# Recurrent attention beside a windowed attention layer: layer B's V, scores and PV in 32-wide TensorE tiles, layer A in tiles of 64 tokens

## The chip, the cores and the metric

One core of a Trainium2 chip runs the whole program. The metric is the device time of one execution in microseconds (us). A profile of one execution gives every instruction's start and end on TensorE (PE, its weight loads PEld), VectorE (DVE), ScalarE (ACT), GpSimd (POOL) and the queues, and the clock that was granted to TensorE.

## The reference

```python
x = A_x                                    # 1 x 2048 x 576, bfloat16
x = x + A(layernorm(x))                    # layers 1 and 3: 32 heads of 18, each token sees
x = x + B(layernorm(x))                    #   itself and 7 earlier tokens, 2 apart
x = x + A(layernorm(x))
x = x + B(layernorm(x))                    # layers 2 and 4: 32 heads of 128
# B, for each of 64 segments of 32 tokens:
h = concat([mem, xs])                      # 8 memory rows + 32 rows of x
q, k, v = h @ Wq, h @ Wk, h @ Wv
p = softmax(mask(q @ k.T * scale)); o = (p @ v) @ Wo
mem = o[:, :8]; outs.append(o[:, 8:])      # the next segment needs mem
```

Layer B is a recurrence: 64 segments, one after the other. Both B layers run together as two "lanes" of one step, the second a few segments behind the first, with 80 columns (2 x 40) on TensorE.

## The kernel before

Some words first. SBUF and PSUM are the memories in which the program keeps its tiles; all its matmuls write to tiles in PSUM. HBM holds its inputs, its results and A's weights. The columns of a matmul are those of the operand that it streams (80 for most of B's). "Scores" are Q x K^T, "PV" is the product of the softmax P with V, which gives O.

The weights of B stay in SBUF. A step of B is a fixed list of blocks; TensorE's order is laid down when the program is built. Between B's blocks a budget lets blocks of layer A in ("generators" that yield a block of matmuls or a gap of time). A's weights aren't kept beside B's: each block of 160 KB is loaded from HBM into a ring of six buffers when it is needed.

```python
def stage_c(g):                    # 4 heads: V transposed back to rows, scores, softmax
    psV = ...                      # matmul(psV[:, hh, :], lhsT=v^T, rhs=ident)
    for hh in range(4):
        nc.tensor.matmul(psS[:, hh, :], lhsT=q, rhs=k, start=True, stop=False)
        nc.tensor.matmul(psS[:, hh, :], lhsT=self.ident[0:NC2, 0:NC2], rhs=self.m80b[:, :], ...)  # mask
    ...                            # max (VectorE), exp (ScalarE, one per head), sum, P = e / sum (GpSimd)
def stage_e(g): ...                # P transposed by TensorE, copied by ScalarE
def stage_g(g): ...                # O = V x P^T
def oproj(g): ...                  # 6 x 80 columns for each head
# --- cut: A's budget
self.a_budget = min(self.a_budget + dt * cfg["a_share"], cfg["a_burst"])   # 0.25, 1.5
while self.agens and self.a_budget > 0:
    ...
    self.a_budget -= cfg["a_blk"]                                          # 0.3 a block
# --- cut: layer A, tiles of TT = 128 tokens
nc.vector.tensor_copy(out=kT[:, :, 0:HALO], in_=hk[:, 0])   # 14 columns of the tile before
nc.vector.tensor_copy(out=vT[:, :, 0:HALO], in_=hk[:, 1])
```

## Time and profile before

| before | |
|---|---|
| median of 3 | 3384.12 us (3382.23 to 3387.86) |
| busy, of the span of 3384.5 us | PE 84%, PEld 78%, DVE 56%, ACT 44%, POOL 44% |
| mean granted clock | 0.971 |
| loads of A's weight blocks | 640 of 160 KB |

Busy shares say which engine leads; the list of waits says for what it stands still. From that list for TensorE (engine, line waited at, engine and line waited for: us in all, times, longest us):

```profile
PE b_psO L624 <- ACT b_PT L616: 70.6, 119, 2.7
PE b_psO L624 <- DVE b_OT L630: 47.3, 81, 0.6
```

```profile
DVE a_kT L298 <- POOL a_prod L335: 66.9, 30, 6.3
```

Inside the steps TensorE's largest waits are for B's own P and O copies; its one long wait for A's weights, 90.0 us, lies before the first step. The line of VectorE's list looks harmless: VectorE, copying the 14 halo columns of K, waits for GpSimd.

### The profile page before, as it was taken

What the parts mean: (1) busy time and instruction counts of PE and PEld (TensorE: products, weight loads), DVE (VectorE), ACT (ScalarE), POOL (GpSimd) and SP (SyncE); (2) the same over time, 40 slices, a digit from 0 to 9 for tenths busy, and PEclk for the clock granted to TensorE, in tenths of its full rate; (3) what the DMA queues carried; (4) which work ended last, traced back from release to release, by engine and by line L of the source; (5) the groups of instructions that cost most, each with busy time, mean ns of one, the idle gap of its engine ahead of it and who ended that gap; (6) DMA issues with size and microseconds to landing.
All of it is one profiled execution on the core that took longest, in us unless ns stands there. A gap on an engine that the chain in (4) does not pass through costs nothing. (4 is left out here: it accounts for less than half of the span.)

```text
span 3384.5 us, 146469 instructions
## 1 busy us (share of the span) xinstructions
PE 2854.0 (84%) x64880; PEld 2627.9 (78%) x64880; DVE 1894.2 (56%) x4387; ACT 1498.5 (44%) x4729; POOL 1474.9 (44%) x2546
## 2 busy tenths in 40 slices
PE   0488888888888988888888888898888898989887
PEld 0388778887888878888878778887888888878887
DVE  2255655655665555555555556565555565656554
ACT  0244444444444444444444444444444444444443
POOL 3455545454554544354545455454535351515111
PEclk9799999999999999999999999999999999999999
DMA  8222112121222222222212122212222120201000
GB/s 290 68 60 73 53 50 63 37 78 47 65 56 65 57 56 57 66 59 62 65 46 70 44 63 56 65 56 56 57 64 59 31 68 13 67 12 50 14 16 10
DMA packets 246960, 198.35 MB, mean 59 GB/s; under 512 B 120884, under 2 KB 230516, under 8 KB 244788
## 3 DMA queue, kind: packets, MB, share of 16 engines
q1 hardware_dynamic: 142724, 163.81, 16.3%
q10 hardware_dynamic: 100352, 6.30, 1.9%
q0 software_dynamic: 3248, 18.88, 1.5%
q8 instruction: 507, 8.31, 1.0%
q14 instruction: 129, 1.06, 0.1%
HBM read 156.02 MB, written 32.90 MB: 56 GB/s over the span
## 5 line engine op out<-in xcount | busy, mean ns | idle before, releaser
L538 PE MATMUL b_psr<-hT,wq 128*128 128x80 bf16 x9216 | 790.3, 201 | 61.4 <-DVE hT L688 17.3
L538 PE MATMUL b_psr<-hT,wv 128*128 128x80 bf16 x9216 | 765.3, 202 | 0.0
L538 PE MATMUL b_psr<-hT,wk 128*128 128x80 bf16 x9216 | 761.7, 202 | 0.0
L603 POOL TENSOR_TENSOR b_P<-b_sm,b_ssum 80x320 bf16<-80x320 bf16 x504 | 361.1, 718 | 915.6 <-DVE b_ssum L601 490.3
L597 ACT ACTIVATE b_sm<-b_psS,b_nmx 80x80 bf16<-80x80 f32 x2304 | 579.0, 323 | 222.2 <-DVE b_nmx L582 152.1
L538 PEld LDWEIGHTS <-wq 128*128 128x128 bf16 x9216 | 555.5, 100 | 102.4 <-issue 93.6
L644 PE MATMUL b_psY<-b_OT,wo 128*128 128x80 bf16 x13824 | 613.6, 208 | 0.0
L644 PEld LDWEIGHTS <-wo 128*128 128x128 bf16 x13824 | 577.7, 104 | 8.0 <-issue 3.0
L545 ACT CAST b_qkv<-b_psr 128x480 bf16<-128x480 f32 x576 | 321.8, 559 | 542.3 <-PE b_psr L541 541.0
L547 DVE CAST b_qkv<-b_psr 128x480 bf16<-128x480 f32 x576 | 374.2, 650 | 275.9 <-PE b_psr L541 270.4
L538 PEld LDWEIGHTS <-wk 128*128 128x128 bf16 x9216 | 513.1, 100 | 0.5 <-issue 0.2
L538 PEld LDWEIGHTS <-wv 128*128 128x128 bf16 x9216 | 509.8, 100 | 1.7 <-issue 1.6
L616 ACT CAST b_PT<-b_psT 80x320 bf16<-80x320 f32 x576 | 243.8, 423 | 523.5 <-PE b_psT L612 504.5
L600 DVE TENSOR_REDUCE b_ssum<-b_sm 80x4 f32<-80x320 bf16 x576 | 275.9, 479 | 354.7 <-ACT b_sm L597 324.5
L541 PE MATMUL b_psr<-hT,wk_r 128*128 128x80 bf16 x2304 | 464.7, 202 | 0.0
L541 PE MATMUL b_psr<-hT,wv_r 128*128 128x80 bf16 x2304 | 464.1, 201 | 0.0
L541 PE MATMUL b_psr<-hT,wq_r 128*128 128x80 bf16 x2304 | 463.6, 201 | 0.0
L569 PE MATMUL b_psS<-b_qkv 128*80 128x80 bf16 x2304 | 364.9, 206 | 98.1 <-ACT b_sm L597 36.2
L335 POOL TENSOR_TENSOR a_prod<-a_t,a_kT 128x1024 bf16<-128x1024 bf16 x160 | 317.2, 1996 | 134.8 <-ACT a_t L312 86.4
L572 PE MATMUL b_psS<-m80b,ident 80*80 80x80 bf16 x2304 | 358.6, 204 | 0.0
L587 DVE CAST b_V<-b_psV 80x512 bf16<-80x512 f32 x504 | 341.7, 678 | 22.9 <-PE b_psV L559 22.7
L569 PEld LDWEIGHTS <-b_qkv 128*80 128x80 bf16 x2304 | 253.5, 118 | 106.4 <-DVE b_qkv L547 69.6
(140 smaller groups left out, 5208.3 us busy)
## 6 DMA issues: line engine op xcount, KB each, us to landing
a_w<-wA_blk SPq DMA_DIRECT2D x640, 160.0 KB, 2.7
x1T<-xres SPq DMA_DIRECT2D x16, 320.0 KB, 3.0
d2T<-b_stg SPq DMA_DIRECT2D x64, 80.0 KB, 1.6
xres<-x1T SPq DMA_DIRECT2D x16, 320.0 KB, 3.3
xres<-d2T SPq DMA_DIRECT2D x16, 320.0 KB, 2.9
x3T<-xres SPq DMA_DIRECT2D x16, 320.0 KB, 3.5
d4T<-b_stg SPq DMA_DIRECT2D x64, 80.0 KB, 1.6
xres<-x3T SPq DMA_DIRECT2D x16, 320.0 KB, 3.3
```

Source lines behind the costliest of these rows:

```text
L335: e_prod.tensor_tensor(out=prod[:], in0=qT[:, c, :].unsqueeze(1).to_broadcast([P, AW, T]), in1=win(kT, c), op=ALU.mult)
L538: last = nc.tensor.matmul(ps[:, hh, wi, :], lhsT=wt[:, kc, h * P:(h + 1) * P], rhs=hT[:, kc, :], start=(kc == 0), stop=False)
L541: last = nc.tensor.matmul(ps[:, hh, wi, :], lhsT=wr[:, hr * P:(hr + 1) * P], rhs=hT[:, 4 + h // (HB // 2), :], start=False, stop=True)
L545: nc.scalar.copy(out=sb[:], in_=ps[:])
L547: nc.vector.tensor_copy(out=sb[:], in_=ps[:])
L569: mm = nc.tensor.matmul(psS[:, hh, :], lhsT=t_[:, hh % 2, 0, :], rhs=t_[:, hh % 2, 1, :], start=True, stop=False)
L572: last = nc.tensor.matmul(psS[:, hh, :], lhsT=self.ident[0:NC2, 0:NC2], rhs=self.m80b[:, :], start=False, stop=True)
L587: nc.vector.tensor_copy(out=V[:], in_=psV[:])
L597: nc.scalar.activation(out=sm[:, hh, :], in_=psS[:, hh, :], func=ACT.Exp, bias=nmx[:, hh:hh + 1], scale=1.0)
L600: nc.vector.tensor_reduce(out=ssum[:], in_=sm[:], axis=AX.X, op=ALU.add)
L603: (nc.vector if crit else nc.gpsimd).tensor_tensor(out=Pm[:], in0=sm[:], in1=ssum[:].unsqueeze(2).to_broadcast([NC2, 4, NC2]), op=ALU.mult)
L644: last = nc.tensor.matmul(psY[:, mb, :], lhsT=self.wo[:, c0:c0 + P], rhs=OTs[g][:, hh, :], start=(ocount[0] == 1), stop=(ocount[0] == 6 * HB))
```

## The change

The intent is less work on TensorE and fewer dependent copies: four 32-wide tiles work at once in V, scores and PV; V comes straight from x as rows (no transposes); P is transposed on VectorE; the x columns go through PV in this step and through the output projection in the next one, so that only the 16 memory columns are urgent. For this the softmax takes all 128 partitions. Layer A's tiles shrink from 128 to 64 tokens, the lanes' delay from 8 to 6 segments (70 steps, not 72).

```diff
-TT = 128
+T = 64
+NS = T // SEG
--- cut
-                psV = self.ps_r.tile([NC2, 4, P], F32, name="b_psV", tag="r")
-            psT = self.ps_a.tile([P, 4, NC2], F32, name="b_psT", tag="TO")
--- cut
+    def vpass(self, t, b, engines):
+            for kc in range(5):
+                for c in range(4):
+                    mm.append(nc.tensor.matmul(ps[c * 32:(c + 1) * 32, :], lhsT=l, rhs=w, start=(kc == 0), stop=(kc == 4)))
--- cut: score_m, score_x, pv_m, pv_x in groups of four tiles
+        nc.vector.transpose(out=pt[:].rearrange("p i b q -> p (i b q)"), in_=e[:].rearrange("p i k -> p (i k)"))
--- cut: the order of a step
+        for g in range(11):
+            seq.append((self.qk, t, g))
+            if g == 6:
+                seq += [(self.vpass, t, 1, ("act", "dve")), (self.score_m, 0), (self.score_x, 0)]
+        seq += [(self.vpass, t, 0, ("act", "act")), (self.score_m, 1), (self.score_x, 1), (self.pv_m, 0),
+                (self.oproj, 0, 12), (self.pv_m, 1), (self.oproj, 12, 16), (self.oproj, 16, 24), (self.oproj, 24, 32),
+                (self.mem_out, t), (self.x_out, t - 1), (self.pv_x,)]
--- cut: A's budget, a block of weights costs 0.15
-        self.a_budget = min(self.a_budget + dt * (cfg["a_share"] if share is None else share), cfg["a_burst"])
+        self.owed = min(self.owed + us, 2.0)
+SHARE = 0.18
```

## The prediction

> **What bounds the kernel now.** I read the page first (busy shares, slices, chain), then the stretches of two steps without and three with layer-A work, then the groups of instructions by shape, the list of waits, and the timeline of single steps.
>
> The page:
>
> ```profile
> PE 2854.0 (84%) x64880; PEld 2627.9 (78%) x64880; DVE 1894.2 (56%) x4387; ACT 1498.5 (44%) x4729; POOL 1474.9 (44%) x2546
> ...
> PE b_psY L644 5%; PE b_psr L538 4%; ACT b_sm L597 3%; DVE b_qkv L547 2%; PE b_psS L569 1%; ACT b_qkv L545 1%; PE b_psr L541 1%; DVE b_V L587 1%; PE b_psO L624 1%; PE b_psT L612 1%; ACT b_PT L616 1%; DVE b_ssum L600 1%; DVE b_nmx L582 1%; PE a_psqkv L308 1%; DVE b_OT L630 1%
> ```
>
> TensorE leads with 84%, and the chain that ended last runs from engine to engine. The program is a recurrence: 72 steps of layer B (64 segments and a delay of 8), each needing the memory columns that the last one put out. Stretches of the timeline, all engines (start and end, length, busy time and count of each engine, clock, DMA):
>
> ```profile
> 0.00:149.20 149.20, 20.74 (x156) 12.16 (x157) 32.80 (x76) 9.35 (x19) 67.18 (x153) 0.87 0.61 201
> 149.20:3375.00 3225.80, 2832.59 (x64719) 2615.28 (x64718) 1859.76 (x4308) 1489.15 (x4710) 1407.69 (x2393) 0.98 0.19 52
> ...
> 3257.80:3296.50 38.70, 34.54 (x833) 32.18 (x833) 20.44 (x47) 16.94 (x56) 5.02 (x7) 1.00 0.02 5
> ...
> 1616.00:1662.40 46.40, 40.04 (x883) 36.35 (x883) 29.22 (x68) 21.47 (x66) 25.29 (x54) 0.96 0.22 58
> ```
>
> About 149 us of loading and the first A tile, 3226 us of steps (44.8 each), 10 us of tail. A step with no A work takes 38.7 us, one with it 44 to 46. A step has 832 matmuls of layer B: 480 projections, 192 output projections, and 160 for V transposes, scores, masks, P transposes and PV. From start to start they are about 36 ns apart (56 for the 32 of N=128), so B's TensorE work is 800 x 36 + 32 x 56 = 30.6 us; A adds on average 3.7 us (counts by start gaps). The remaining 8 us without A and 10 to 11 with it are waits. Where they lie, from the timeline of the step without A:
>
> ```profile
> 3288.80 1.89 PE L644 MATMUL b_psY<-b_OT,wo 128*128 128x80 bf16 x48
> ...
> 3292.40 0.32 PE L612 MATMUL b_psT<-ident,b_P 80*80 80x80 bf16 x4
> 3292.81 0.42 ACT L616 CAST b_PT<-b_psT 80x320 bf16<-80x320 f32 x1 [1.45 <-PE b_psT L612]
> 3293.28 0.30 PE L624 MATMUL b_psO<-b_PT,b_V 80*128 80x80 bf16 x4 [0.56 <-ACT b_PT L616]
> 3293.62 0.49 DVE L630 CAST b_OT<-b_psO 128x320 bf16<-128x320 f32 x1 [3.01 <-PE b_psO L624]
> 3294.17 0.30 PE L624 MATMUL b_psO<-b_PT,b_V 80*128 80x80 bf16 x4 [0.58 <-DVE b_OT L630]
> ```
>
> 48 matmuls less the 0.2 us of one's length give 36 ns each; then TensorE waits 0.56 us for each copy of P or O: the softmax chain of the last head groups has too little work laid over it.
>
> [...] A's logits already use four 32-column tiles:
>
> ```profile
> 1691.11 0.29 PE L340 MATMUL a_psL<-a_prod,epad 128*32 128x256 bf16 x4
> 1714.19 0.39 PE L373 MATMUL a_psB<-a_e,epadT 32*128 32x256 bf16 x4
> ```
>
> Four matmuls of N=256 are done in 0.29 us, where one takes 0.285: they start 3 ns apart. In single records about 130 ns pass into and 210 ns out of such a group, of which 107 is streaming: some 100 ns per change of mode. The second line has two row tiles twice: the second pair starts 120 ns after the first, so a group costs its streaming time plus 13 ns. [...] (min/median/max in ns):
>
> ```profile
> L603 DVE TENSOR_TENSOR b_P<-b_sm,b_ssum x72: 424/489/1458, 187.7 to 3367.6; 80x320 bf16<-80x320 bf16 x72
> ```
>
> [...]
>
> **The change, TensorE work of a B step.** Q and K: 320 x 36 ns = 11.5 us. V: 6 half passes of 5 groups of four N=512 tiles, (512/2.4 + 13) ns a group, 6 x 1.13 = 6.8 (before 160 x 36 ns plus 32 transposes of 56 = 7.5). Scores with masks: groups of four at 36 + 13 = 50 ns; mask groups 146 and 173 ns; 2 x (0.35 + 0.57) = 1.8 (before 64 x 36 = 2.3). P transposes: gone (1.15). PV: 12 + 12 + 24 groups of 50 ns = 2.4, more than the 1.15 before. Output: 160 x 36 = 5.8 (192 before: 6.9). Nine changes of mode: 0.9. Sum 29.2 us, against 30.6. So the tiles themselves save only 1.4 us a step. A tiles of 64 tokens: per tile 100 matmuls of N=64 (29 ns, 2.9 us), 10 of N=128 for the norms (0.6), logits 0.6, spread 0.5, transposes 0.2: 4.8 us x 64 / 70 steps = 4.4 us (before 3.7). Together 33.6 us a step, before 34.3.
>
> **What is worth more: waits.** The softmax takes all 128 partitions, with 16 heads an instruction: exp 576 x 4 pieces of 0.32 us become 280 of about 0.45; the copy of P^T on ScalarE goes; V is copied from two passes that don't need memory. The x columns' PV and the V pass of the next step's second lane stand between the last output matmul and the next Q/K: 1.2 + 2.3 us over the 0.6 us in which memory returns. That wait (0.5 us) is gone. VectorE gets more: per step 5 QK copies 3.3, one V copy 0.7, max/add/sum/reciprocal/multiply/transpose 2 x 2.6 + 2 x 2.5, O copies 2.2, memory 0.6, together 17 us, plus A 7.7: 25 of some 39 us. No engine but TensorE is at its limit.
>
> I followed two steps by hand through the built order, with these durations. Four waits came out. (a) The first PV's copy of O stands on VectorE behind max, add, sum and reciprocal of the second score half, ready 3.4 us after those scores; TensorE is there after 1.6: 1.8 us before the output matmuls. (b) PSUM: Q/K, V, scores and A's products now share three buffers; behind the first score half a Q/K group waits for an exp or for a copy that VectorE does after the softmax: 2 to 3 us. (c) A's spread and PV share one buffer of four banks: 1.6 us where they meet. (d) Less than 0.5 elsewhere. The two walks ended at 40.6 and 41.2 us; both were dense in A work, and without A I get 34. I take 33.6 + 5.2 = 38.8.
>
> **Forced tiles.** In the built order of TensorE, from step 17 on every sixth step, eight times, logits, spread, output and norm of one A tile stand back to back: the next segment needs it. The chain: softmax 2.0, spread and its copies 2.8, V multiplies 1.6, GpSimd adds 4.5 (slope of the before kernel's adds), residual and norm 1.5: some 11 us of waiting each.
>
> **Sum.** Start 140 (A tile smaller, weights the same), 62 steps x 38.8 = 2406, 8 x 50 = 400, tail 15 (one more output projection, then the last tile): 2961, so 2960 us, 12.5% less. Of the gain of 424, two steps fewer give 90, the rest is waits.
>
> **Rivals.** R1, waits fully hidden: 33.6 us a step, 70 x 33.6 + 155 = 2507, or 2600 with forced tiles. For it: the work is there to fill with. Against: TensorE runs in one fixed order, and the before kernel with the same freedom keeps 10 us. R2, VectorE becomes the bound in the score stretches, as its two-input multiplies are shut out by GpSimd (1400 instead of 489 ns in 16 of 72 cases) and every copy queues behind them: 3 us more a step, 3170. Against: only 3 to 5 of its instructions a step have two SBUF inputs. R3, tile groups of small N don't keep 50 ns[...]. The trace shows groups of four only singly, so it can't be ruled out. R4, weight traffic doubles (1280 blocks of 160 KB instead of 640, some 205 MB): the mean DMA share is 19%, so 40% at most; hidden.
>
> **Range and chances.** A walk of dependent waits may miss by 2.5 us a step: 2760 to 3160. Slower than before would need 46 us a step, R2 and R3 together and more: faster 0.94, same 0.04, slower 0.02.
>
> **What would show it.** Steps of about 39 us and eight of about 50; V groups 226 ns apart; TensorE's wait for the first O copy near 1.8 us; waits of Q/K matmuls on VectorE copies; no wait at the step's border. Wrong if small groups are slower than 50 ns, if the transposes take over 1 us, or if the waits at shared PSUM are under 3 us or over 8.

## More of the kernel before

The page's row of the clock (tenths, 40 slices) is full:

```profile
PEclk9799999999999999999999999999999999999999
```

## The result, and the profile after

| | before | after |
|---|---|---|
| median | 3383.18 us (3381.19 to 3387.86) | 3582.65 us (3575.53 to 3590.58) |
| granted clock | 0.971 | 0.880 |
| steps | 72 | 70 |

The kernel became slower: ratio 1.0588 (95% interval 1.0563 to 1.0613). Ratios here are the mean time of one kernel's fast runs over that of the other's of the same rounds, so not quite the ratio of the medians. The result lies 623 us above the prediction. The page after:

```profile
PE 2646.4 (74%) x73360; PEld 2213.0 (62%) x73360; DVE 1583.8 (44%) x3949; ACT 1051.7 (29%) x2317; POOL 1007.2 (28%) x1007
...
PEclk9998889898979879897897988989899799978899
```

No engine is busier than before: the time went into waiting, and the clock has holes. TensorE's and VectorE's largest waits inside the steps now:

```profile
PE b_psY L601 <- DVE OT L560: 181.2, 93, 4.3
PE a_psqkv L290 <- DMA a_w<-wA_blk: 111.5, 119, 3.7
...
PE b_psqk L452 <- DVE b_qk L461: 69.0, 40, 6.7
PE a_psY L373 <- POOL a_o L367: 57.3, 9, 6.4
```

```profile
DVE a_k L284 <- POOL a_big L310: 221.3, 55, 9.3
```

Three of the five are layer A's. The tiles themselves do what they should; from the timeline of one step (start us, us, engine, line, operation, count):

```profile
1595.76 1.05 PE L484 MATMUL b_psv<-wv,hT 128*32 128x512 bf16 x16
1596.63 0.39 PE L484 MATMUL b_psv<-wv_r,hT 128*32 128x512 bf16 x4
...
1598.07 0.32 PE L516 MATMUL b_psm<-b_qk 128*32 128x80 bf16 x16
1598.21 0.34 PE L530 MATMUL b_psx<-mask_x,ident 128*32 128x384 bf16 x4
```

From start to start, 16 V matmuls take 0.87 us, 217 ns for a group of four; 16 score matmuls take 0.14 us, 35 ns a group.

**A ledger of TensorE's time.** I split the time from start to start of its matmuls, from the first step (149.2 us before, 132 us after) to the last matmul, into: columns at full clock (columns / 2.4 ns, a group of four tiles counted once; at full clock matmuls of 80, 128 and 256 columns start 36, 56 and 109 ns apart in the trace before, 2.4 columns a ns between them, and at half clock those of 80 and 128 start 67 and 107 ns apart in the trace after, 1.2 a ns; the clock records of both have only the levels 1.0 and 0.5); what half clock adds; gaps of over 150 ns beyond that, by the matmul that ends them; and the rest. (The parts exceed the time, by up to 2.2% in the tables of this document, where neighbouring matmuls overlap; trust the rest least.)

| us | length | columns | half clock | gaps ahead of A | gaps ahead of B | rest |
|---|---|---|---|---|---|---|
| before | 3231 | 2294 | 61 | 91 | 510 | 276 |
| after | 3443 | 1941 | 278 | 411 | 538 | 320 |

The work fell by 353 us. Gaps ahead of A's blocks took 320 of it back, the clock 217. By steps: those with A work take 46.9 us in the mean, except the eight in which a whole A tile was forced through in front of the step (75.9 us); predicted were 38.8 and 50.

### The profile page after: what moved, and what is told of

Same layout as the page of the kernel before. It is cut to its first block, busy times and chain, and to the rows that moved or that the text cites.

```text
span 3579.8 us, 159066 instructions
## 1 busy us (share of the span) xinstructions
PE 2646.4 (74%) x73360; PEld 2213.0 (62%) x73360; DVE 1583.8 (44%) x3949; ACT 1051.7 (29%) x2317; POOL 1007.2 (28%) x1007
## 5 line engine op out<-in xcount | busy, mean ns | idle before, releaser
L452 PE MATMUL b_psqk<-hT,wq 128*128 128x80 bf16 x8960 | 729.9, 209 | 171.6 <-DVE b_qk L461 69.0
L452 PE MATMUL b_psqk<-hT,wk 128*128 128x80 bf16 x8960 | 729.0, 209 | 0.0
L601 PE MATMUL b_psY<-OT,wo 128*128 128x80 bf16 (+1 forms) x11360 | 551.8, 222 | 182.0 <-DVE OT L560 181.2
L484 PE MATMUL b_psv<-wv,hT 128*32 128x512 bf16 x6720 | 476.1, 405 | 43.7 <-DVE b_qk L461 31.3
L454 PE MATMUL b_psqk<-hT,wq_r 128*128 128x80 bf16 x2240 | 467.5, 209 | 0.1
L454 PE MATMUL b_psqk<-hT,wk_r 128*128 128x80 bf16 x2240 | 467.0, 208 | 0.0
L310 POOL TENSOR_TENSOR a_big<-a_q,a_k 128x1024 bf16<-128x1024 bf16 (+1 forms) x192 | 320.1, 1692 | 134.6 <-ACT a_k L296 132.8
L290 PE MATMUL a_psqkv<-a_xn,a_w 128*128 128x64 bf16 x4800 | 260.9, 202 | 130.4 <-DMA a_w<-wA_blk 111.5
L454 PEld LDWEIGHTS <-wq_r 128*128 128x128 bf16 x2240 | 234.4, 105 | 0.0
L454 PEld LDWEIGHTS <-wk_r 128*128 128x128 bf16 x2240 | 234.0, 104 | 0.0
```

What stands on the lines that cost most here:

```text
L290: mm = [nc.tensor.matmul(ps[:, c, :], lhsT=w[:, kc, :], rhs=xn[:, kc, :], start=(kc == 0), stop=(kc == 4)) for kc in range(5)]
L310: nc.gpsimd.tensor_tensor(out=big[:, c0:c0 + nb], in0=qT[:, c0:c0 + nb].unsqueeze(2).to_broadcast([P, nb, AW, T]), in1=win(kT, c0, nb), op ...
L452: mm.append(nc.tensor.matmul(ps[:, hh, wi, :], lhsT=wt[:, kc, h * P:(h + 1) * P], rhs=hT[:, kc, 0:W80], start=(kc == 0), stop=False))
L454: mm.append(nc.tensor.matmul(ps[:, hh, wi, :], lhsT=wr[:, (h % 16) * P:(h % 16 + 1) * P], rhs=hT[:, 4 + h // 16, 0:W80], start=False, stop ...
L484: mm.append(nc.tensor.matmul(ps[c * 32:(c + 1) * 32, :], lhsT=l, rhs=w, start=(kc == 0), stop=(kc == 4)))
L601: mm.append(nc.tensor.matmul(self.psY[:, mb, c0:], lhsT=self.wo[:, w0:w0 + P], rhs=self.OT[:, h, c0:], start=(h == 0 and mb == 0), stop=(h ...
```

## The experiments

Every edit is on the changed kernel unless another is named.

**1. The queue of the weight loads.** B's loads and stores stand on the same queue as A's weight loads; they go to ScalarE's.

```diff
-            self.nc.sync.dma_start(out=hT[:, :, XC[lane]:XC[lane] + SEG], in_=self.xnT[lane][:, s])
+            self.nc.scalar.dma_start(out=hT[:, :, XC[lane]:XC[lane] + SEG], in_=self.xnT[lane][:, s])
```
(and the two stores alike)

> Only edit: the x loads, the stores of the layer-B output and the final stores are issued from ScalarE's queue, so that A's weight loads stand behind fewer waits in the SyncE queue. Weight theory (286 us more than streaming time in A's projections, because their blocks stand in one queue behind stores that wait for the step's end): the wait of A's projections falls from 286 us above streaming to under 150, half-clock share from 0.25 to 0.18-0.21, time 3350 to 3480. Rival (the pace of issue and a ring of six buffers sets the wait, not the queue's order): within 1% of 3583.

Measured: 3623.37 us, ratio 1.0703 (1.0687 to 1.0719), slower than the change itself. TensorE's wait for weights at A's projections stayed at 111.5 us in all, so waits at the head of that queue are not what holds the weights up. What became longer are the waits of Q/K matmuls for ScalarE, from 91 to 142 us; the likely reason, not tested, is that ScalarE's own instructions now stood behind those transfers' waits.

**2. PV earlier.** PV of the first half goes ahead of the second half's scores, so that its O copy isn't behind their softmax on VectorE.

```diff
-(self.score_m, 1), (self.score_x, 1), (self.pv_m, 0),
+(self.pv_m, 0), (self.score_m, 1), (self.score_x, 1),
```

> Only edit: the first PV half is put before the second score half, so that its copy stands ahead of that softmax on VectorE. Stall theory: the wait of the output projection for the copy of O (128 us above streaming) nearly goes, and the clock drops that it sets off (33 of 136) too: time 3583 minus 125 minus about 60, 3370 to 3440, half-clock share about 0.20. Rival (TensorE then only waits at the second PV instead, as the softmax of the second score half has less over it): wait moves, time over 3520.

Measured: 3549.37 us, ratio 1.0482 (1.0441 to 1.0523): 33 us. Most of the wait moved: ahead of the output projection it fell from 181 to 77 us for VectorE's copies, and 90 us of such waits appeared ahead of PV. It is a small term.

**3. Does the clock count?** 28 idle multiplications fill the wait for the first O copy, once with 112 columns each, once (control) with 4.

```diff
-                (self.oproj, 0, 12),
+                (self.warm, 28, 112), (self.oproj, 0, 12),
```

> Only edit: 28 idle matmuls of 112 columns (1.4 us at full clock) into spare columns of the output bank, in the wait between the first PV and the output projection; nothing else moves. Clock theory[...]: drops set off at that place (33 of 136) mostly go, half-clock share 0.25 to about 0.19, time 3583 to 3480-3540 although there is more work on TensorE. Rival (clock plays no part, or it is a matter of temperature or load): same or slower, 3583 to 3650.

> Control of the run with idle matmuls: the same 28 at the same place with 4 columns each (112 columns in all[...]). If columns streamed count, the clock isn't helped: half-clock share within 0.02 of 0.25, time 3560 to 3620. If the number of matmuls or TensorE's being occupied counts, as the run with 112 columns.

Measured: 3552.25 us with 112 columns (ratio 1.0494, 1.0474 to 1.0513; clock 0.894) and 3578.14 with 4 (1.0575, 1.0549 to 1.06; clock 0.879). More work made the kernel faster, and only if it had columns. The windows at half clock fell from 252 to 222 (in the clock records before and after the change, every drop and return lies on one grid of 3413 ns; a window is one stretch of it). So the clock is a real term, but a loss that follows from waits.

**4. The forced tiles.** A's share of B's clock goes from 0.18 to 0.22; in the order of TensorE no A tile is then forced.

```diff
-SHARE = 0.18
+SHARE = 0.22
```

> One constant of the changed kernel: layer A may take 0.22 instead of 0.18 of layer B's clock. In the order of TensorE's instructions no A tile is then performed as a whole block in front of a step any more (in the changed kernel eight steps have one, 17, 23 to 59, at 73 to 79 us against about 47 for their neighbours). Theory (the budget of A was just too small, and the tile that came due was performed as one chain whose waits nothing covers): eight times about 28 us fall, 3340 to 3400 us, ratio 0.99 to 1.005. Rival (A's waits are only moved from the eight steps into the sixty others, because what waits is data and weights, not the order): 3530 to 3590 us, as the changed kernel.

Measured: 3433.75 us, ratio 1.0149 (1.0134 to 1.0164): 149 us less, between the two expectations. The eight steps fell from 75.9 to 48.2 us, but the others, which took over the work, rose from 46.9 to 48.4. How a forced tile spends its time, from the changed kernel's timeline (in brackets the wait and what ended it):

```profile
1604.27 0.46 PE L318 MATMUL a_psL<-a_big,epad 128*32 128x128 bf16 x20
1608.69 0.61 PE L339 MATMUL a_psB<-a_e,epadT 32*128 32x128 bf16 x16 [3.95 <-DVE a_e L330]
1612.11 0.29 PE L339 MATMUL a_psB<-a_e,epadT 32*128 32x128 bf16 x4 [2.81 <-DVE a_big L352]
1618.78 1.49 PE L373 MATMUL a_psY<-a_o,a_w 128*128 128x64 bf16 x25 [6.37 <-POOL a_o L367]
1621.70 0.58 PE L226 MATMUL ln_ps<-ln_xs,ones 128*128 128x128 bf16 x4 [1.44 <-ACT ln_xs L222]
```

These four waits are 14.6 us. On the way the clock has dropped: the 25 matmuls of 64 columns start 53 ns apart, where those of the burst at 1634.20, shown under 5, start 29 ns apart.

**5. The bursts.** A may claim 0.75 us at once, not 2.0, with a budget large enough (0.30) that nothing is forced; then the control, that budget with the old cap.

```diff
-        self.owed = min(self.owed + us, 2.0)
+        self.owed = min(self.owed + us, 0.75)
-SHARE = 0.18
+SHARE = 0.3
```

> Budget 0.30 and a cap of 0.75 us instead of 2.0 on what A may claim at once: no forced tile, and layer A's projection blocks stand at most 5 in a row on TensorE (25 instructions) where the changed kernel has runs of 14 blocks, which need more weight blocks than the six buffers hold. Theory (bursts run ahead of the weight loads, 0.37 us a block on the queue against 0.15 us on TensorE): below the run with the budget alone by 60 to 150 us. Rival (the waits are for data of the layer norm and for VectorE, and more, shorter visits cost more changes): same as the budget alone within 1%, or slower.

> Control of the cap: budget 0.30 with the cap left at 2.0 us, so no forced tile, but runs of 11 and 14 blocks on TensorE. Theory (the length of the bursts counts): as with budget 0.22 or worse, 3420 to 3480 us. Rival (the larger budget itself made the gain of the cap's run): 3310 to 3350.

Measured: 3321.22 us (ratio 0.9826, 0.9795 to 0.9858) with the short cap, 3500.02 (1.0354, 1.0339 to 1.0369) with the long one. The length of the bursts alone is worth 180 us. Why, from the changed kernel's timeline of a run of fourteen blocks:

```profile
1634.20 1.04 PE L290 MATMUL a_psqkv<-a_xn,a_w 128*128 128x64 bf16 x30
1638.89 1.70 PE L290 MATMUL a_psqkv<-a_xn,a_w 128*128 128x64 bf16 x20 [3.65 <-DMA a_w<-wA_blk]
1640.96 0.93 PE L290 MATMUL a_psqkv<-a_xn,a_w 128*128 128x64 bf16 x10 [0.37 <-DMA a_w<-wA_blk]
```

The first six blocks, as many as the ring holds, run through; then TensorE waits for loads that couldn't start before one of the six buffers was free again. In this trace one block's load takes 0.38 us of the queue's time to issue (median of 1280) and 3.1 us from there to landing; TensorE's five matmuls for it take 0.15 us. TensorE's wait for weights in the two runs, with the long cap and with the short one:

```profile
PE a_psqkv L290 <- DMA a_w<-wA_blk: 185.7, 259, 3.0
```

```profile
PE a_psqkv L290 <- DMA a_w<-wA_blk: 39.6, 43, 2.3
```

**6. No weight loads** (wrong result): six blocks, loaded at the start, stay in SBUF and are used again and again, once in the changed kernel's order, once with short bursts.

```diff
-        w = self.ring.tile([P, 5, P], BF16, name="a_w")
-        self.nc.sync.dma_start(out=w[:], in_=self.wA[i])
-        return w
+        self.n_w += 1
+        return self.wres[self.n_w % 6]
```

> Wrong result on purpose: layer A's weight blocks are loaded once, six of them, and used again and again, so there are no weight loads in the steps. Order as in the changed kernel, forced tiles too. Theory (the wait for weight blocks is a large part of A's 13 us per step): the 390 us of waits ahead of A's projections fall to under 150, the time to 3330 to 3430 us. Rival (the weights wait only because nothing else comes later; without them TensorE waits there for A's data instead): 3500 to 3580 us.

> Wrong result on purpose: budget 0.30 with the cap of 0.75 us, and layer A's weight blocks resident (no loads in the steps). In the long bursts taking the loads away gave 163 us. Theory (short bursts had already brought that gain, since the loads then keep up): less than 60 us below 3321, 3265 to 3320. Rival (loads cost the same in either order, by traffic or by the queue): another 100 to 160 us, 3160 to 3220.

Measured: 3420.01 us (ratio 1.0104, 1.0078 to 1.0129), 163 us less; and 3241.52 (0.9575, 0.9555 to 0.9595), 80 us less than the short bursts with loads. The second lies between the two expectations: the loads cost half as much in the order with short bursts, and still cost something. (The two orders differ in A's budget and in the forced tiles too.)

**7. The x columns in their own step**, one part of the change undone.

```diff
-                (self.mem_out, t), (self.x_out, t - 1), (self.pv_x,)]
+                (self.mem_out, t), (self.x_out, t)]      # and pv_x, pv_m(1) straight after pv_m(0)
```

> One part of the change undone, on the changed kernel: the x columns go through PV and the output projection in their own step, not one later. TensorE then has PV of the x columns and its four copies between the first half's PV and the output matmuls in every step, and nothing but the V pass at the step's border. Theory (the delay takes work off the path between scores and memory): 2 to 4 us a step longer, 3720 to 3870 us. Rival (A's interleaving sets the steps, so that the delay is hidden anyway): 3550 to 3620.

Measured: 3879.15 us (ratio 1.1474, 1.1458 to 1.1489), 297 us more. So the delay of the x columns is worth some 4 us a step, with two things in it that weren't separated: the second half's PV also moved ahead of the first output matmuls, and the clock fell to 0.830. PV then stands in the path of every step, its operand behind VectorE:

```profile
PE b_psox L581 <- DVE b_ptx L543: 207.6, 70, 7.8
PE b_psom L556 <- DVE OT L590: 190.6, 70, 2.8
```

**8. Layer B alone, and with parts of A** (wrong results). In the first, A computes its first tile only and hands its normalised x to B for all others. In the second, all of A's TensorE instructions are there in the changed kernel's order, on operands that stay in place. In the third, all of A's other instructions are there, but for the weight loads, and read a constant instead of PSUM. The first edit, its main lines:

```diff
+    def a_tile(self, layer, j):                      # B alone
+        if layer == 1 and j == 0:
+            yield from self.a_real(layer, j)
+            return
+        self.nc.sync.dma_start(out=self.xnT[...][:, NS * j:NS * j + NS], in_=self.xnb[0][:])
```

> Wrong result on purpose: layer B as in the changed kernel, layer A only for its first tile, whose normalised x every later tile hands to B (one transfer each). No A work stands in the steps. Prediction's step of 34 us without A right: 132 + 70 x 33.5 + 46 = 2520 us, 2480 to 2580, nearly no half-clock windows. Rival (the five steps without A at the end, 32 to 34 us, were short because one of their two lanes was empty): 2650 and more.

> Wrong result on purpose: as B alone, but every instruction of layer A on TensorE is there, in the changed kernel's order (the eight tiles in one chain too), on operands that stay in place: A waits for no data, no weights and no copies, and the other engines do nothing for it. Prediction's 4.4 us of A on TensorE right: about 70 x 4.4 = 310 us above B alone, 2780 to 2880. Rival (the visits themselves[...] make A's 13 us a step): 3100 and more.

> Wrong result on purpose: layer A without TensorE. All its instructions on VectorE, ScalarE and GpSimd and its transfers except the weight loads are there and read a constant in place of the products. What it takes above B alone is what A does to B's copies and softmax on those engines. If A's cost were mainly the waits of TensorE in A's own blocks: 2560 to 2700 us. Rival (VectorE and ScalarE, in order, make B's copies wait behind A): 2800 to 3000.

Measured: B alone 2399.0 us, less than expected (ratio 0.7089, 0.7067 to 0.711), with A's TensorE work 2804.32 (0.8283, 0.8269 to 0.8297), with A's other engines 3084.11, more than expected (0.9114, 0.91 to 0.9128). The page of B alone:

```profile
PE 2059.0 (86%) x63595; PEld 1751.1 (73%) x63595; DVE 1098.5 (46%) x2500; ACT 656.8 (27%) x1277; POOL 161.3 (7%) x249
...
PEclk9999999999999999999999999999999999999999
```

B alone has steps of 32.4 us, and A's TensorE work, in the same order of matmuls as in the changed kernel, makes them 38.7. That this is the number predicted for everything is chance: B came out below its 34 and A's matmuls above their 4.4. What remains to 3583 us, 778 us, is neither B nor A's work on TensorE. It is what A's data, its loads and its work on the other engines add: waits, and the clock that falls with them (0.968 here, 0.880 in the changed kernel). The third run is of limited use: with no TensorE blocks to tie them down, A's instructions were ordered otherwise and crowded into the first 14 steps (66 to 71 us each; the later ones about 36). It shows that A on VectorE, ScalarE and GpSimd can double a step of B, not how much it did in the changed kernel.

**9. Does A's TensorE work count in its place?** On the first run of experiment 6, of each chain of five matmuls only one is left (wrong result).

```diff
-rhs=xn[:, kc, :], start=(kc == 0), stop=(kc == 4)) for kc in range(5)]
+rhs=xn[:, kc, :], start=True, stop=True) for kc in range(1)]
```
(and in the norms, logits and output)

> Wrong result on purpose: on the run with resident weights (3420 us), of every chain of five accumulating matmuls of layer A only the first is left, in projections, norms, logits and output; everything else (order, copies, softmax, transfers) stands. TensorE's columns for A fall to about a quarter. Theory (what A costs beyond its 405 us of TensorE time alone is waits for data and B's copies behind A's on the other engines, and the matmuls partly lie in those waits): less than 200 us gained, 3220 to 3330. Rival (A's TensorE work is additive): about 300 us gained, 3080 to 3160.

Measured: 3369.56 us (ratio 0.9949, 0.9915 to 0.9984), 50 us less than 3420.01, fewer than either theory had. By the split of the ledger 175 us of columns went (1941 to 1766), while gaps of over 150 ns grew by some 70 us and half clock took another 70 (224 windows at half clock against 185). So A's matmuls aren't additive, but the run doesn't show that they all lie beside waits: as much as the waits took back, the clock took, likely because there was less to stream; no run tested that.

**10. Candidates.** First the parts of 2, 3 and 4 together; then those of 2 and 5; then 2, 3 and 5.

> A candidate: budget 0.22, PV of the first half ahead of the second half's scores, and 28 idle multiplications of 112 columns in the wait for the first O copy. The three parts alone have given or are expected to give about -220, -34 and -31 us against the changed kernel; if they add up 3300 us, and if what they remove overlaps 3340 to 3400. Rival that the budget does nothing: 3520 us.

> The candidate (3266 us) without its idle multiplications: budget 0.30, cap 0.75, PV of the first half earlier. If the idle multiplications pay through the clock as on the changed kernel (31 us): 3290 to 3310. Rival (the reordering made all of it): 3240 to 3270.

> A candidate: budget 0.30 with the cap of 0.75 us (3321 us alone), PV of the first half ahead of the second half's scores, and the 28 idle multiplications of 112 columns in the wait for the first O copy. On the base with budget 0.22 the last two gave 31 us together (3434 to 3403). If they add up here too: 3280 to 3300 us, ratio 0.97 to 0.976, with about 100 us less wait at the output matmuls and fewer half-clock windows. Rival (with bursts this short nothing is left of the clock's loss at that place, and the 91 us of extra columns are paid in full): 3330 to 3370.

Measured: 3402.63 us (ratio 1.0059, 1.0044 to 1.0074), 3292.83 (0.9724, 0.97 to 0.9749) and 3265.85 (0.9664, 0.9637 to 0.9692). The earlier PV and the idle multiplications still give 28 and 27 us by the medians, 35 and 20 by the ratios (each run's to its own runs of before).

**11. One copy moved.** In the third candidate's timeline VectorE and, last line, TensorE:

```profile
1237.93 0.71 DVE L543 STREAM_TRANSPOSE b_ptx<-ex 128x512 bf16<-128x512 bf16 x1 [1.88 <-POOL ex L503]
1240.91 0.19 DVE L284 COPY a_k<-a_halo 128x70 bf16<-128x70 bf16 x1 [2.27 <-POOL a_big L310]
1241.02 0.65 DVE L461 CAST b_qk<-b_psqk 128x480 bf16<-128x480 f32 x1
...
1241.72 1.28 PE L484 MATMUL b_psv<-wv,hT 128*32 128x512 bf16 x16 [3.47 <-DVE b_qk L461]
```

The copy of the halo columns into the next tile's K takes 0.19 us, but it waits 2.27 us until GpSimd's multiplies have read the old K. B's Q/K copy is queued behind it, and the V pass on TensorE waits 3.47 us for that copy, because it needs its PSUM buffer. The list of waits names only the copy that came last, b_qk; the cause is the instruction ahead of it. The edit puts the halo copy on GpSimd, where it stands behind those multiplies in the program.

```diff
-            nc.vector.tensor_copy(out=kT[:, :, 0:HALO], in_=hk[:, 0])
+            nc.gpsimd.tensor_copy(out=kT[:, :, 0:HALO], in_=hk[:, 0])
```

> The candidate (3266 us) with one instruction moved: the copy of 14 halo columns into the next tile's K goes from VectorE to GpSimd. In the candidate's trace this copy of 0.19 us stands on VectorE for 2.3 us, waiting until GpSimd's multiplies have freed K, and B's Q/K copy queued behind it keeps TensorE from the V pass for 3.6 us, 27 times (97 us). Theory (a waiting A instruction at the head of an in-order engine is what B pays for): 3160 to 3210 us, the wait at the V pass gone. Rival (the wait moves to the next copy): 3245 to 3280.

Measured: 3152.58 us (3147.88 to 3156.84), correct, ratio 0.9316 (0.9298 to 0.9333), 113 us less for one word. By the split of the ledger gaps ahead of B's blocks fell by some 70 us, and half clock by some 45 with them. The wait at the V pass in the candidate, and in this run, and then this run's page:

```profile
PE b_psv L484 <- DVE b_qk L461: 96.6, 30, 3.5
```

```profile
PE b_psv L484 <- DVE b_qk L461: 29.5, 29, 2.6
```

```profile
PE 2541.8 (81%) x75320; PEld 2134.1 (68%) x75320; DVE 1647.0 (52%) x3887; ACT 1035.3 (33%) x2317; POOL 1019.7 (32%) x1069
...
PEclk9999999999999999999999999999999999999999
```

The clock is back at 0.973. This version beats both kernels. It has everything that the change has (tiles, transposes on VectorE, the delay of the x columns, 64-token tiles), another order around it, and 28 idle multiplications a step, without which the clock was lower in the candidates too (0.936 against 0.957).

## Why the prediction was wrong

The ledgers of the decisive runs beside that of the changed kernel:

| us | length | columns | half clock | gaps ahead of A | gaps ahead of B | rest |
|---|---|---|---|---|---|---|
| after | 3443 | 1941 | 278 | 411 | 538 | 320 |
| B alone | 2268 | 1693 | 79 | 0 | 296 | 249 |
| B, and A on TensorE | 2669 | 1941 | 81 | 61 | 303 | 334 |
| short bursts | 3182 | 1941 | 195 | 165 | 585 | 345 |
| last candidate | 3015 | 2033 | 68 | 163 | 445 | 350 |

**Right: layer B's tiles and its step.** Predicted were V groups of 226 ns and small groups of 50; the trace has 217 and 35, so rival R3 fell. The transposes on VectorE take 567 and 711 ns, under the 1 us above which the prediction called itself wrong; no trace had one before, so what its sum for VectorE holds for them was the author's estimate. Wait (a), for the first O copy, was put at 1.8 us; with B alone it is 159.2 us in 70 steps, 2.3 each. Wait (b), of Q/K matmuls at the shared PSUM buffers, was put at 2 to 3 us: TensorE stood 166 us there in the changed kernel, 2.4 a step, but with B alone only 0.7, so most of it comes with A. "Without A I get 34": 32.4 with B alone.

**Mis-sized: A's work on TensorE.** 4.4 us a step was predicted. It costs 38.7 less 32.4, 6.3 us, even when it waits for no data: the columns are 248 us in all, 4.1 for each of some 60 steps, and small gaps and waits at the shared PSUM buffer make up the rest.

**Wrong: "I take 33.6 + 5.2 = 38.8".** This is the step that failed. B's own waits are about 3 us (32.4 less the predicted work of 29.2), so 5.2 left some 2 for the coupling with A. From 38.7 with A's TensorE work alone to 46.9 in the plain steps, it is 8. Over 52 such steps 46.9 instead of 38.8 makes 421 us of the 623 missed. The four waits that came out of the walks by hand are waits of B's blocks and for PSUM; none is a wait of A's blocks for their weights or data. (5.2 also lies under both walks, dense in A work, which ended 7.0 and 7.6 above 33.6.) The runs show three things in their place.

- *Weights.* The prediction looked at the mean DMA share ("40% at most; hidden", R4). The share stayed at 29%, and the loads still cost 163 us (experiment 6), since a run of fourteen blocks meets a ring of six. A mean share doesn't tell whether a supply keeps up with a burst.
- *A at the head of an engine in order.* In experiment 11 a ready B copy stood behind a waiting A copy for 2.3 us: the last Q/K matmul ended at 1238.25, VectorE was idle from 1238.64 to 1240.91, then A's copy ran, and after it B's. The prediction counted VectorE's work, "25 of some 39 us", and concluded that it was not a limit; it is 44% busy, and still TensorE's largest wait in the steps is for one of its copies (181.2 us). Twice as many tiles make such waits more frequent: in the changed kernel VectorE stood at that one copy for 221.3 us in 55 tiles, before the change for 66.9 in 30. That experiment was made on the candidate; in the changed kernel its worth wasn't measured.
- *The clock.* The prediction took full clock. Half clock cost 278 us of TensorE's time, before 61. It isn't a cause of its own but goes with the waits: 949 us of gaps in the changed kernel, 750 with short bursts (half clock 195), 608 in the last candidate (68, with its idle multiplications), 296 with B alone (79).

**Wrong in size: the forced tiles.** Eight were predicted, and eight there are, but with 11 us each; they cost 75.9 less 46.9, 29 us. The chain's five waits (3.95, 2.81, 6.37, 1.44 and another norm's 0.96) are 15.5 us; what follows runs at half clock and meets a burst of projections. Against the predicted 50 us a step that is 207 us. The remaining steps, start and tail nearly cancel: the first step starts at 132 us (predicted 140), and the last one starts 46.5 us before the end; less a step of 32 that leaves a tail of 14 (predicted 15).

**The other rivals.** R2, VectorE's two-input multiplies held up by GpSimd, occurs but is small. In the changed kernel's trace 18 of the 140 multiplies of the first line below took over 1.4 times the median (1000 ns in their middle, not 482); all 18 overlap a tensor operation of GpSimd, and none of the other 122 does. In the trace before, the P multiply of the prediction did so 17 times in 72 (16 of them at 1381 to 1458 ns), overlapping one each time (8 more overlapped one and kept their time). No group of 50 or more instructions that read PSUM or a single SBUF tile has one over 1.4 times its median in either trace: the 77 Q/K copies and 48 transposes of 512 columns that overlap one of GpSimd's in the changed kernel's stay within 2%. The multiply concerned, after and with B alone (min/median/max in ns):

```profile
L503 DVE TENSOR_TENSOR em<-em,b_summ x140: 479/482/1507, 155.8 to 3555.5; 128x320 bf16<-128x320 bf16 x140
```

```profile
L494 DVE TENSOR_TENSOR em<-em,b_summ x140: 479/481/483, 147.7 to 2385.9; 128x320 bf16<-128x320 bf16 x140
```

Its sum is 79 us against 67; the norm's small multiply of two SBUF operands (L233, median 226 ns, longest 1820) lost some 20 more. In the last candidate the two lose about 80 us of VectorE's time together; what that costs the run wasn't tested. R1, with all waits hidden, is far off.

**What stays open.** From 2804 us (B with A's TensorE work) to the last candidate, 3153, some 350 us remain, 92 of them the columns of the idle multiplications, as far as they don't lie in waits. Of the rest I have shown the 80 us of weight loads on a neighbouring version. How the remainder divides between A's data waits and other B copies queued behind A isn't settled. That A now shares three PSUM buffers with B, where it had two of its own, may be part of it; no run tested that.

## What to carry to other kernels

When two streams of work share engines in order, as VectorE was here (2.3 us ahead of a ready copy in experiment 11), price a visit by what its first waiting instruction holds up, not by its busy time; look for short instructions with a long wait ahead of a ready one, and put them on the engine that they wait for. A budget for filling in work needs a cap shorter than the buffers behind it can feed, and enough share that nothing is ever forced. Measure each layer alone before judging a change to both: here the rewrite was good and its interleaving hid that.

## What else the traces show

- The clock, counted in the changed kernel's trace. Its 276 clock records begin on one grid of 3413 ns, to within 6 ns. I counted the columns streamed in each window of that grid (a tile as a quarter): the 136 drops in the steps follow windows of at most 3200 columns, median 1664, and the returns follow half-clock windows of at least 3008. The line isn't sharp: 13 of 622 other full-clock windows had 3200 or fewer (down to 2784) with no drop after them, and 8 of 114 half-clock ones had 3008 or more with no return. Idle multiplications of 112 columns brought the stretches at half clock from 138 to 103, as many with 4 columns left 139.
- Small tiles. In the changed kernel's trace, at full clock, a whole group of four column tiles takes 25 ns from start to start at 48 columns (median) and 35 at 80, 9 ns a matmul.
- Transposes on VectorE. 384 columns took 567 ns and 512 took 711: a line through both, my estimate, has 1.1 ns a column and 135 ns of start.
- A wait whose named releaser was itself queued behind another stream's instruction: the list gave 96.6 us to b_qk, and moving a_k's copy took 113 us off the run.
